# Zero matmuls in more of TensorE's planned gaps, layernorm statistics kept in planned order, and a reordered tail, in a fused attention and FFN kernel

## The chip, the core and the metric

The kernel runs on one core of a Trainium2 chip, as one launch. Its time is the device time of that launch in microseconds (us), lower is better. Five engines share the work, each with its own queue of instructions: TensorE (PE, with its weight loads PEld), VectorE (DVE), ScalarE (ACT), GpSimd (POOL) and SyncE (SP, which here only issues DMAs).

## The reference, cut to what matters

```python
xn = _layernorm(x, axis=-1)            # x: 1 x 2048 x 512, bf16
s = _A_ref(xn, A_wq, A_wk, A_wv, A_wo) # 32 query heads of width 16, one key/value head
g = _silu(_B_ref(xn, B_w_gate, B_w_up, B_w_down))   # SwiGLU FFN, width 1792
return x + s * g

# _A_ref: q = x @ wq (32 heads), k = x @ wk, v = x @ wv
# p = softmax(q k^T / 4) over all 2048 keys; o = p v; o @ wo
# _B_ref: (silu(x @ w_gate) * (x @ w_up)) @ w_down
```

## The kernel before

**The work.** Scores are made transposed, 128 keys by 512 queries, for four heads at once. A pair is 512 queries of eight heads (16 pairs); a pair is done in two blocks of four heads (31 blocks that end with an eviction, and a last one). A block has 16 key tiles. For each tile PE writes scores into two of three two-bank PSUM tiles `ring` (L895), ACT takes the exponential of 1024 columns into a buffer `Pb` (L916, 838 times), and PE adds probabilities times values into `o_ps` (L790). The value weights also hold columns of ones, so `o_ps` carries the softmax's denominators. For 186 of the 1024 half tiles DVE takes the place of ACT: one pass into `Ub` (L928) and, for each two of them, four more passes (L941, L944, L947, L950) whose results `Eb` and `Wb` go into `o_ps` too. At a block's end DVE copies `o_ps` to `oa` (L834), SP sends the denominators to `dn` (L837), and after a pair DVE takes their reciprocal (L724), which goes through DRAM and comes back broadcast as `rb`; POOL multiplies (L735).

**The filling.** The FFN (L654, L674), the queries of the next pair (L515) and the output projection (L690) use a single PSUM bank `m_ps`, one group of matmuls after another, with ACT and DVE work between.

**The order.** It is written by a planner, `_Sched` (L180), at build time: operations carry a cost, dependences and a priority; the planner lets time run, picks for each engine what comes next, and the instructions are emitted in the order of their planned starts. `chain` (L524) then ties each engine's instructions in that order, in one chain per engine. An instruction that is not passed to `chain` is placed by the framework's own scheduler.

**Zero matmuls.** `warm_op` (L739) makes a matmul of a zero weight tile, 512 columns wide, into `o_ps`; it changes no sum. `step` (L255) asks for one when PE would stand idle in the plan for over 0.25 us and the planner's count of PE work over its last `WIN` falls below `LOW`:

```python
if self.warm and start - self.free["PE"] > 0.25 and self.activity(start) < self.LOW:
    ...
    w = self.warm()
    if w is not None and start - max(t, w.ready) > 0.25:
```

`o_rel[0]` is the operation after which `o_ps` may be written anew, which is the block's last copy L834. It is set when the planner comes to the block's last tile (`finish_block`, L825), and until that copy is planned `warm_op` gives nothing.

**The start.** x arrives in tiles of 128 rows. `e_stats` (L436) does the statistics of one tile, BN_STATS (L437) and then BN_AGGR (L438), and returns the second only. Then come the variance plus epsilon (L441), the power -0.5 on POOL (L444), the normalized tile (L455 on DVE for the first four tiles, L451 on POOL for the others), transposes (L466), queries, keys and the first scores.

**The tail.** The last block's four query tiles of 128 rows are finished outside the planner (L995 to L1038), and nothing of that is passed to `chain`: the projection of what is ready (L1002, L1004), the copy of `o_ps` on ACT (L1012), denominators by a matmul (L1015), and for each tile in turn reciprocal, broadcast on DVE, transpose (L1018 to L1021), product (L1022) and the last projection (L1023); then `e_out_mul` (L694), `e_out_add` (L699) and the stores on SP. Last comes a flag (L1031 to L1038): whether all denominators are in range. All engines load it (L1041) and branch over a slower exact path.

## Time and profile before

| what | value |
|---|---|
| time, three runs | 900.57, 905.36, 1078.65 us; median 905.36 us |
| profiled execution, its own time | 903.82 us |
| its span, first to last instruction | 902.0 us |
| mean granted TensorE clock | 0.937 |
| busy: PE, ACT, DVE, POOL | 811.8, 819.9, 711.1, 69.2 us |

The profiled execution lies between the two faster runs. Times in the trace count from the span's start. The granted clock is 1.00 at TensorE's upper level (2.4 GHz) and 0.50 at its lower one (1.2 GHz); for a stretch it is the mean. Matmuls are pipelined and their ends are modelled, so PE's busy time overlaps and is not PE at its peak.

### The profile page before, as it was taken

What the parts mean: (1) busy time and instruction counts of PE and PEld (TensorE: products, weight loads), DVE (VectorE), ACT (ScalarE), POOL (GpSimd) and SP (SyncE); (2) the same over time, 40 slices, a digit from 0 to 9 for tenths busy, and PEclk for the clock granted to TensorE, in tenths of its full rate; (3) what the DMA queues carried; (4) which work ended last, traced back from release to release, by engine and by line L of the source; (5) the groups of instructions that cost most, each with busy time, mean ns of one, the idle gap of its engine ahead of it and who ended that gap; (6) DMA issues with size and microseconds to landing.
All of it is one profiled execution on the core that took longest, in us unless ns stands there. A gap on an engine that the chain in (4) does not pass through costs nothing.

```text
span 902.0 us, 15161 instructions
## 1 busy us (share of the span) xinstructions
PE 811.8 (90%) x5899; PEld 242.2 (27%) x5899; DVE 711.1 (79%) x856; ACT 819.9 (91%) x921; POOL 69.2 (8%) x81
## 2 busy tenths in 40 slices
PE   5899989999989889999999999899998989899984
PEld 2322222222222222222222322222222222222222
DVE  6367887888788996887777988978777998877873
ACT  1999897999999998998989999999998999999981
POOL 4400100000001100000000120000000020000001
PEclk7998896999999997998979999999988999999987
DMA  9200000000000000000000010000000010000000
GB/s 331 66 4 8 12 1 20 1 9 13 4 17 13 25 7 19 2 2 19 1 19 1 13 32 1 19 1 20 2 8 13 7 31 8 19 2 8 13 14 27
DMA packets 20367, 18.78 MB, mean 21 GB/s; under 512 B 9088, under 2 KB 16256, under 8 KB 20288
## 3 DMA queue, kind: packets, MB, share of 16 engines
q1 hardware_dynamic: 18704, 17.18, 6.1%
q8 instruction: 48, 0.79, 0.4%
q10 hardware_dynamic: 1584, 0.56, 0.2%
q14 instruction: 31, 0.25, 0.1%
HBM read 12.88 MB, written 2.36 MB: 17 GB/s over the span
## 4 chain that ended last, share of the span: by engine, by line
PE 43%; ACT 25%; DVE 18%; issue 9%; DMA 2%; SPq 2%; ACTq 0%; DVEq 0%
ACT Pb L916 24%; PE ring L895 17%; PE o_ps L790 11%; DVE Ub L928 7%; PE m_ps L654 6%; PE m_ps L674 4%; DVE Wb L950 2%; DVE Wb L947 2%; SPq L837 2%; DMA dn<-oa 1%; DVE Eb L944 1%; PE o_ps L747 1%; DVE Wb L941 1%; ACT th L659 1%; PE m_ps L690 1%
## 5 line engine op out<-in xcount | busy, mean ns | idle before, releaser
L916 ACT ACTIVATE Pb<-ring 128x1024 bf16<-128x1024 f32 x838 | 790.4, 1085 | 41.1 <-PE ring L895 37.7
L895 PE MATMUL ring<-QB,KT 32*128 32x512 bf16 x2048 | 343.4, 398 | 46.6 <-ACT Pb L916 33.8
L928 DVE TENSOR_SCALAR Ub<-ring 128x1024 uint16<-128x1024 f32 x186 | 227.2, 1222 | 106.9 <-PE ring L895 85.4
L790 PE MATMUL o_ps<-Pb,VA 128*32 128x512 bf16 x1676 | 209.1, 406 | 0.2 <-ACT Pb L916 0.2
L895 PEld LDWEIGHTS <-KT 32*128 32x128 bf16 x2048 | 101.0, 91 | 335.5 <-issue 330.1
L950 DVE TENSOR_TENSOR Wb<-Wb,Ub 128x2048 f16<-128x2048 f16 x93 | 115.1, 1237 | 2.1
L947 DVE TENSOR_TENSOR Wb<-Wb 128x2048 f16<-128x2048 f16 x93 | 114.6, 1232 | 0.0
L790 PE MATMUL o_ps<-Ub,VD 128*32 128x512 f16 x372 | 77.0, 411 | 0.6 <-DVE oa L834 0.4
L654 PE MATMUL m_ps<-xnT,wu_sb 128*128 128x512 bf16 x224 | 71.6, 412 | 3.9 <-DVE ab L661 3.5
L735 POOL TENSOR_TENSOR oT<-oa,rb 128x512 bf16<-128x512 f32 x16 | 24.2, 1511 | 632.2 <-DMA rb<-dscr 491.9
L790 PEld LDWEIGHTS <-VA 128*32 128x32 bf16 x1676 | 50.6, 94 | 81.5 <-issue 81.3
L654 PE MATMUL m_ps<-xnT,wg_sb 128*128 128x512 bf16 x224 | 69.2, 404 | 1.3 <-DVE hT L665 0.6
L674 PE MATMUL m_ps<-wd_sb,hT 128*128 128x512 bf16 x224 | 66.8, 390 | 1.2 <-DVE g_sb L682 0.9
L941 DVE TENSOR_SCALAR Wb<-Ub 128x2048 uint16<-128x2048 uint16 x93 | 65.0, 699 | 1.6
L944 DVE TENSOR_SCALAR Eb<-Ub 128x2048 uint16<-128x2048 uint16 x93 | 64.8, 697 | 0.0
L790 PEld LDWEIGHTS <-VD 128*32 128x32 f16 x1116 | 40.7, 93 | 82.3 <-issue 80.2
L665 DVE TENSOR_TENSOR hT<-ab,m_ps 128x512 bf16<-128x512 f32 x56 | 38.1, 681 | 12.8 <-PE m_ps L654 12.2
L790 PE MATMUL o_ps<-Wb,VD 128*32 128x512 f16 x372 | 38.7, 406 | 7.1 <-DVE Wb L950 6.4
L661 DVE SCALAR_TENSOR_TENSOR ab<-th,m_ps 128x512 f32<-128x512 f32 x56 | 38.1, 681 | 8.7 <-ACT th L659 8.7
L790 PE MATMUL o_ps<-Eb,VD 128*32 128x512 f16 x372 | 38.4, 403 | 7.1 <-DVE Eb L944 6.5
L659 ACT ACTIVATE th<-m_ps 128x512 f32<-128x512 f32 x56 | 36.6, 654 | 4.6 <-PE m_ps L654 4.6
L699 POOL TENSOR_TENSOR xn<-ab,x_sb 128x512 bf16<-128x512 f32 x14 | 20.3, 1450 | 165.7 <-DVE ab L694 165.7
(93 smaller groups left out, 298.3 us busy)
## 6 DMA issues: line engine op xcount, KB each, us to landing
rb<-dscr SPq DMA_DIRECT2D x16, 256.0 KB
out_dram<-xn SPq DMA_DIRECT2D x16, 128.0 KB, 1.7
dn<-oa SPq DMA_DIRECT2D x124, 2.0 KB, 1.7
oa<-oa SPq DMA_DIRECT2D x60, 32.0 KB, 2.0
wg_sb<-in_B_w_gate_dram SPq DMA_DIRECT2D x1, 1792.0 KB, 12.1
wu_sb<-in_B_w_up_dram SPq DMA_DIRECT2D x1, 1792.0 KB
wd_sb<-in_B_w_down_dram SPq DMA_DIRECT2D x1, 1792.0 KB, 19.2
...
```

What stands on the lines that cost most here:

```text
L654: return lambda: [nc.tensor.matmul(out=m_ps[:], lhsT=w[:, kc, f * P:(f + 1) * P], rhs=xnT[:, kc, sc * 512:(sc + 1) * 512], start=(kc == 0) ...
L659: t_ = OP("ACT", 0.48, [a], lambda: nc.scalar.activation(out=th[i][:], in_=m_ps[:], func=ACT.Tanh, scale=0.5), (0,), name="tanh")
L661: s_ = OP("DVE", 0.62, [t_, ab_rel[i]], lambda: nc.vector.scalar_tensor_tensor(out=ab[i][:], in0=th[i][:], scalar=1.0, in1=m_ps[:], op0=AL ...
L674: return lambda: [nc.tensor.matmul(out=m_ps[:, :D], lhsT=hT[:, f, tt * P:(tt + 1) * P], rhs=wd_sb[:, f, :], start=(f == 0), stop=(f == FC ...
L790: r.append(nc.tensor.matmul(out=o_ps[GRP * g:GRP * g + GRP, :], lhsT=lhs, rhs=rhs, start=(n == 0), stop=(n == pv_total[(b, g)] - 1), tile_ ...
L895: return [nc.tensor.matmul(out=ring[sl][:, u * 512:(u + 1) * 512], lhsT=KT[half][GRP * g:GRP * g + GRP, t * P:(t + 1) * P], rhs=QB[pair % ...
L916: ex = OP("ACT", 0.905, [scs[x], pdep, prev_exp], lambda i=i, sl=sl: nc.scalar.activation(out=Pb[i][:], in_=ring[sl][:], func=ACT.Exp, sca ...
L928: pa = OP("DVE", 1.16, [scs[dx]] + udep, lambda ui=ui, x=dx, sl=sl: nc.vector.tensor_scalar(out=Ub[ui][:, x * 1024:(x + 1) * 1024], in0=ri ...
L941: e1 = OP("DVE", 0.62, [pa, pa0, edep], lambda ui=ui, ei=ei: nc.vector.tensor_scalar(out=Wb[ei][:], in0=Ub[ui][:], scalar1=0x3FF, scalar2= ...
L944: e2 = OP("DVE", 0.62, [pa, pa0, edep], lambda ui=ui, ei=ei: nc.vector.tensor_scalar(out=Eb[ei][:], in0=Ub[ui][:], scalar1=0x7C00, scalar2 ...
L947: e3 = OP("DVE", 1.18, [e1], lambda ei=ei: nc.vector.tensor_tensor(out=Wb[ei][:].bitcast(FP16), in0=Wb[ei][:].bitcast(FP16), in1=Wb[ei][:] ...
L950: e4 = OP("DVE", 1.18, [e3], lambda ui=ui, ei=ei: nc.vector.tensor_tensor(out=Wb[ei][:].bitcast(FP16), in0=Wb[ei][:].bitcast(FP16), in1=Ub ...
```

## The change

There are four edits. (1) `LOW` goes from 3300 to 3600. (2) `warm_op` gives a zero matmul also between `finish_block` and the block's copy: into `o_ps` while some of the block's matmuls are still to come, and, when they are all planned, into `m_ps` if a group of matmuls there is begun and not ended. `finish_block` hands the last block's matmuls to the same test. (3) `e_stats` and `e_flag1` return all their instructions, so that all of them are chained. (4) The tail is written in another order and chained: the copy of `o_ps` is split between ACT and DVE, the broadcasts go to ACT, reciprocals and products take two tiles at once, the flag is worked out before the outputs, and two of the four stores are issued from ACT.

```diff
-    WIN, LOW = 3.0, 3300
+    WIN, LOW = 3.0, 3600
...
     def e_stats(n):
-        nc.vector.bn_stats(out=stats[:, n, :], in_=x_sb[:, n, :])
-        return nc.vector.bn_aggr(out=mv[:, n, :], in_=stats[:, n, :])
+        return [nc.vector.bn_stats(out=stats[:, n, :], in_=x_sb[:, n, :]),
+                nc.vector.bn_aggr(out=mv[:, n, :], in_=stats[:, n, :])]
...
     def grp_pe(parts, prio, paced=False):
...
+        grp = []
+        m_cur.append(grp)
+        while m_cur[0] and m_cur[0][-1].start is not None:
+            m_cur.pop(0)
...
             last = sd.add(o)
+            grp.append(o)
...
     def warm_op():
         ev = o_rel[0]
-        if ev.start is None:
-            return None
+        rdy = 0.0
+        dst = o_ps
+        if ev.start is not None:
+            rdy = ev.end + sd.LAT["DVE"]
+        elif all(d.start is not None for d in ev.deps if d.eng == "PE"):
+            if not any(len(f_) > 1 and f_[0].start is not None and f_[-1].start is None for f_ in m_cur):
+                return None
+            dst = m_ps
...
-            st_ = not any(acc_open)
-            return nc.tensor.matmul(out=o_ps[:], lhsT=zeros_w[:], rhs=KT[0][:, 0:512] if late else QB[1][:],
+            st_ = dst is o_ps and not any(acc_open)
+            return nc.tensor.matmul(out=dst[:], lhsT=zeros_w[:], rhs=KT[0][:, 0:512] if late else QB[1][:],
...
         if b == 2 * NPAIR - 1:
             st["last_pv"] = pvs
-            o_rel[0] = _Op("EXT", 0.0, [], None, (0,))
+            o_rel[0] = _Op("EXT", 0.0, [p_ for p_ in pvs], None, (0,))
...
+    t_acc(0)
+    chain("ACT", nc.scalar.copy(out=oe[:, qsl(0, 2)], in_=o_ps[:, qsl(0, 2)]))
+    chain("DVE", nc.vector.tensor_copy(out=oe[:, qsl(2, 2)], in_=o_ps[:, qsl(2, 2)]))
     for i in range(4):
...
+        t_dq(i)
+    t_acc(1)
+    t_rec(0, 2)
+    t_rec(2, 2)
...
     for i in range(4):
...
+        t_rdx(i)
+    t_rq(0)
+    t_rq(1)
+    t_acc(2)
+    t_rq(2)
+    t_rq(3)
+    t_mul(0, 2)
+    chain("PE", nc.tensor.transpose(out=m_ps[0:1, 0:P], in_=fmin[:, 3:4], identity=ident_f[:]))
+    t_acc(3)
+    t_mul(2, 2)
     for i in range(4):
...
+        t_wom(i)
...
+    chain("DVE", nc.vector.tensor_single_scalar(out=flag_i[:], in_=fm2[0:1, 0:1], scalar=0.5, op=ALU.is_lt))
     for i in range(4):
+        chain("DVE", e_out_mul(NL + i, accs[i], tmps[i]))
+    for i in range(4):
+        pool_ = i < 2
+        chain("POOL" if pool_ else "DVE", e_out_add(NL + i, tmps[i], nc.gpsimd if pool_ else nc.vector))
+        q_ = "SP" if i % 2 == 0 else "ACT"
```

In the new tail `t_acc` is the projection of what is ready for one query tile (four matmuls, as L1002 and L1004), `t_dq` the denominators (L1015), `t_rec` the reciprocal (L1018), `t_rdx` the broadcast (L1019, now on ACT), `t_rq` its transpose (L1021), `t_mul` the product (L1022) and `t_wom` the last projection (L1023).

In the whole program before the exact path PE has 94 zero matmuls before the change and 187 after it. All 187 write `o_ps`; none writes `m_ps`. The changed kernel's line numbers are up to 46 higher.

**DVE at the start.** From the first variance operation to the first normalized tile, before:

```order
L441 TENSOR_SCALAR veps<-mv 128x2
L437 BN_STATS stats<-x_sb 128x6
L441 TENSOR_SCALAR veps<-mv 128x2
L438 BN_AGGR mv<-stats 128x2 x2
L437 BN_STATS stats<-x_sb 128x6 x2
L351 TENSOR_SCALAR hbit<-pidx 128x1
L437 BN_STATS stats<-x_sb 128x6
L353 TENSOR_SCALAR hmask<-hbit 128x1
L354 TENSOR_SCALAR hmask<-hbit 128x1
L437 BN_STATS stats<-x_sb 128x6 x4
L455 TENSOR_SCALAR xn_116<-x_sb,mv,rstd 128x512
```

The same stretch of DVE after the change:

```order
L441 TENSOR_SCALAR veps<-mv 128x2 x2
L437 BN_STATS stats<-x_sb 128x6
L438 BN_AGGR mv<-stats 128x2
L437 BN_STATS stats<-x_sb 128x6
L438 BN_AGGR mv<-stats 128x2
L351 TENSOR_SCALAR hbit<-pidx 128x1
L353 TENSOR_SCALAR hmask<-hbit 128x1
L354 TENSOR_SCALAR hmask<-hbit 128x1
L455 TENSOR_SCALAR xn_116<-x_sb,mv,rstd 128x512
```

Eight BN_STATS stood between the first variance operation and the first normalized tile, and two stand there now; the six others come later, in pairs, between the copies of the transposes.

**PE at a block's end.** The scores of a new block (`KT_84` with `QB_120`) just ahead of the last product of the block that ends (`Pb_126`), at the place that the trace of before has at 344.8 us; before:

```order
L895 LDWEIGHTS KT_84
L895 MATMUL ring_98<-QB_120,KT_84 128x512
L895 LDWEIGHTS KT_84
L895 MATMUL ring_96<-QB_120,KT_84 128x512
L895 LDWEIGHTS KT_84
L895 MATMUL ring_96<-QB_120,KT_84 128x512
L790 LDWEIGHTS VA
L790 MATMUL o_ps<-Pb_126,VA 32x512
```

The same place of PE after the change:

```order
L907 LDWEIGHTS KT_84
L907 MATMUL ring_98<-QB_120,KT_84 128x512
L759 LDWEIGHTS zeros_w
L759 MATMUL o_ps<-KT_84,zeros_w 128x512
L759 LDWEIGHTS zeros_w
L759 MATMUL o_ps<-KT_84,zeros_w 128x512
L907 LDWEIGHTS KT_84
L907 MATMUL ring_96<-QB_120,KT_84 128x512
```

Two zero matmuls stand between the two pairs of score matmuls, where none stood.

**DVE in the tail.** From the product of the third query tile to the flag, before:

```order
L1022 TENSOR_TENSOR oT_151<-oa_143,ring_98 128x128
L1031 TENSOR_SCALAR rb_144<-ring_98 128x16
L1032 TENSOR_TENSOR rb_144<-rb_144,ring_98 128x16
L694 SCALAR_TENSOR_TENSOR oa_140<-ring_97,g_sb 128x512
L694 SCALAR_TENSOR_TENSOR oa_141<-ring_97,g_sb 128x512
L699 TENSOR_TENSOR xn_118<-oa_140,x_sb 128x512
L699 TENSOR_TENSOR xn_119<-oa_141,x_sb 128x512
L1033 TENSOR_REDUCE fmin<-rb_144 128x1
L1034 TENSOR_REDUCE fmin<-fmin 128x1
L1037 TENSOR_REDUCE fm_8151<-m_ps 1x1
L1038 TENSOR_SCALAR flag_i<-fm_8151 1x1
```

And DVE after the change, from the two products to the end of the tail:

```order
L1043 TENSOR_TENSOR oT_151<-oa_143,ring_98 128x256 x2
L1075 TENSOR_REDUCE fm_8183<-m_ps 1x1
L1076 TENSOR_SCALAR flag_i<-fm_8183 1x1
L700 SCALAR_TENSOR_TENSOR ab_138<-ring_96,g_sb 128x512
L700 SCALAR_TENSOR_TENSOR ab_139<-ring_96,g_sb 128x512
L700 SCALAR_TENSOR_TENSOR oa_140<-ring_97,g_sb 128x512
L700 SCALAR_TENSOR_TENSOR oa_141<-ring_97,g_sb 128x512
L705 TENSOR_TENSOR xn_118<-oa_140,x_sb 128x512
L705 TENSOR_TENSOR xn_119<-oa_141,x_sb 128x512
```

The flag is now ahead of the output products and sums, and the last work of DVE is the last sum.

## Rows read from the trace of the kernel before

**Rows 1.** The page: span; granted clock in 40 equal slices, in tenths.

```profile
span 902.0 us, 15161 instructions
...
PEclk7998896999999997998979999999988999999987
```

**Rows 2.** Groups by line: shapes, count | busy us, mean ns | idle before, releaser.

```profile
L916 ACT ACTIVATE Pb<-ring 128x1024 bf16<-128x1024 f32 x838 | 790.4, 1085 | 41.1 <-PE ring L895 37.7 <-PE o_ps L790 1.9 <-ACT Pb L916 0.3
...
L747 PE MATMUL o_ps<-KT,zeros_w 128*128 128x512 bf16 x74 | 28.8, 412 | 0.0
```

**Rows 3.** Half-clock windows: length, busy by engine (instructions), clock, DMA share, GB/s.

```profile
348.00:361.60 13.60, 13.60 (x65) 2.47 (x63) 9.57 (x13) 10.14 (x11) 1.27 (x1) 0.50 0.12 31
...
409.40:416.20 6.80, 6.80 (x34) 1.02 (x32) 3.41 (x4) 2.38 (x4) 1.26 (x1) 0.50 0.16 46
...
860.00:866.80 6.80, 6.45 (x35) 1.22 (x34) 4.47 (x5) 2.67 (x4) 1.27 (x1) 0.50 0.13 41
sum 88.80, PE 88.45 PEld 15.96 DVE 61.78 ACT 61.08 POOL 9.64; mean PE 11.06 PEld 2.00 DVE 7.72 ACT 7.64 POOL 1.20
```

**Rows 4.** Windows between those, at full clock, from 95.4 to 860 us: sum of seven.

```profile
sum 696.30, PE 636.07 PEld 193.31 DVE 583.07 ACT 682.43 POOL 34.75; mean PE 90.87 PEld 27.62 DVE 83.30 ACT 97.49 POOL 4.96
```

**Rows 5.** Timeline of PE, then DVE, at one block's end: start, us, what [idle before].

```profile
344.76 0.39 PE L895 MATMUL ring<-QB,KT 32*128 32x512 bf16 x2
346.06 0.39 PE L895 MATMUL ring<-QB,KT 32*128 32x512 bf16 x2 [0.91 <-ACT Pb L916]
...
348.28 0.68 DVE L834 COPY oa<-o_ps 128x512 f32<-128x512 f32 x1
```

**Rows 6.** Timeline at two places where PE waits longer: DVE, PE, DVE.

```profile
407.97 0.35 DVE L724 RECIPROCAL rc<-dn 128x32 f32<-128x32 f32 x1 [2.01 <-DMA dn<-oa]
...
408.92 0.40 PE L790 MATMUL o_ps<-Eb,VD 128*32 128x512 f16 x4 [1.75 <-DVE Eb L944]
...
859.40 0.35 DVE L724 RECIPROCAL rc<-dn 128x32 f32<-128x32 f32 x1 [2.78 <-DMA dn<-oa]
```

**Rows 7.** Who waited for whom, whole span: us in total, times, longest.

```profile
PE ring L895 <- ACT Pb L916: 33.8, 108, 1.0
```

**Rows 8.** Timeline at the start: DVE, POOL, ACT.

```profile
11.84 2.46 DVE L437 BATCH_NORM_STATS2 stats<-x_sb 128x6 f32<-128x512 bf16 x4
14.22 1.37 DVE L455 TENSOR_SCALAR xn<-x_sb,mv,rstd 128x512 bf16<-128x512 bf16 x4
...
9.26 1.40 POOL L444 TENSOR_TENSOR rstd<-veps,neg_half 128x2 f32<-128x2 f32 x2 [4.15 <-DVE veps L441]
...
16.54 1.01 POOL L444 TENSOR_TENSOR rstd<-veps,neg_half 128x4 f32<-128x4 f32 x1 [5.87 <-DVE veps L441]
...
22.65 7.44 ACT L916 ACTIVATE Pb<-ring 128x1024 bf16<-128x1024 f32 x8 [2.47 <-PE ring L895]
```

**Rows 9.** Timeline of the tail, all engines.

```profile
881.73 0.39 PE L790 MATMUL o_ps<-Pb,VA 128*32 128x512 bf16 x2
...
884.87 0.95 PE L1015 MATMUL ring<-sel,oa 128*128 128x4 f32 x8
...
887.37 0.23 DVE L1019 COPY oa<-rc 128x128 f32<-128x128 f32 x1
...
887.65 0.49 PE L1021 MATMUL ring<-ident_f,oa 128*128 128x128 f32 x2
...
889.85 2.26 POOL L699 TENSOR_TENSOR xn<-ab,x_sb 128x512 bf16<-128x512 f32 x2 [23.41 <-DVE ab L694]
...
890.49 0.60 DVE L1019 COPY oa<-rc 128x128 f32<-128x128 f32 x1
...
893.04 1.29 DVE L694 SCALAR_TENSOR_TENSOR oa<-ring,g_sb 128x512 f32<-128x512 f32 x2 [0.41 <-PE ring L1023]
894.24 1.28 DVE L699 TENSOR_TENSOR xn<-oa,x_sb 128x512 bf16<-128x512 f32 x2
...
896.58 0.14 DVE L1038 TENSOR_SCALAR flag_i<-fm 1x1 int32<-1x1 f32 x1
```

More of the change, by code (lines that the diff above doesn't have):

```diff
@@ L563 @@
     npaced = [0]
+    m_cur = []
     def grp_pe(parts, prio, paced=False):
@@ L750, in warm_op @@
         o.left = 0
-        o.ready = ev.end + sd.LAT["DVE"]
+        o.ready = rdy
         return o
@@ L998 @@
     qpar = (NSC - 1) % 2
-    for i in range(4):
-        n = NL + i
-        for jj in range(jl):
-            nc.tensor.matmul(out=accs[i], lhsT=oT[qpar][:, jj, i * P:(i + 1) * P], rhs=wo_sb[:, jj, :],
-                             start=(jj == 0), stop=False)
-        nc.tensor.matmul(out=accs[i], lhsT=oT[qpar][:, jl, i * P:(i + 1) * P], rhs=wom[0][:],
-                         start=(jl == 0), stop=False)
     oe = oa[3]
@@ L1034, with qsl @@
-    nc.vector.tensor_reduce(out=fmin[:, 3:4], in_=fmin[:, 0:3], axis=AX.X, op=ALU.min)
-    nc.tensor.transpose(out=m_ps[0:1, 0:P], in_=fmin[:, 3:4], identity=ident_f[:])
-    fm2 = sb([P, 2], FP32, "fm2")
-    nc.vector.tensor_reduce(out=fm2[0:1, 0:1], in_=m_ps[0:1, 0:P], axis=AX.X, op=ALU.min)
-    nc.vector.tensor_single_scalar(out=flag_i[:], in_=fm2[0:1, 0:1], scalar=0.5, op=ALU.is_lt)
+    tmps = [ab[0], ab[1], oa[0], oa[1]]
+    fl = rb[0]
+    fm2 = sb([P, 2], FP32, "fm2")
+    def qsl(i, n=1):
+        return slice(i * P, (i + n) * P)
@@ new lines, in t_acc, with t_dq @@
+    def t_acc(i):
+        for jj in range(jl):
+            chain("PE", nc.tensor.matmul(out=accs[i], lhsT=oT[qpar][:, jj, qsl(i)], rhs=wo_sb[:, jj, :],
+                                         start=(jj == 0), stop=False))
+        chain("PE", nc.tensor.matmul(out=accs[i], lhsT=oT[qpar][:, jl, qsl(i)], rhs=wom[0][:],
+                                     start=(jl == 0), stop=False))
+    def t_dq(i):
+        chain("PE", nc.tensor.matmul(out=dq[:, 4 * i:4 * i + 4], lhsT=oe[:, qsl(i)], rhs=sel[:], start=True, stop=True))
@@ new lines, in t_rec, with t_rdx, t_rq @@
+    def t_rec(i, n):
+        chain("DVE", nc.vector.reciprocal(out=rd4[:, 4 * i:4 * (i + n)], in_=dq[:, 4 * i:4 * (i + n)]))
+    def t_rdx(i):
+        chain("ACT", nc.scalar.copy(out=oa[2][:, qsl(i)].rearrange("p (g r) -> p g r", r=GRP),
+                                    in_=rd4[:, 4 * i:4 * i + 4].rearrange("p (g o) -> p g o", o=1).to_broadcast(
+                                        [P, 4, GRP])))
+    def t_rq(i):
+        chain("PE", nc.tensor.matmul(out=rq[:, qsl(i)], lhsT=oa[2][:, qsl(i)], rhs=ident_f[:], start=True, stop=True))
@@ new lines, in t_mul, with t_wom @@
+    def t_mul(i, n):
+        chain("DVE", nc.vector.tensor_tensor(out=oT1[:, qsl(i, n)], in0=oe[:, qsl(i, n)], in1=rq[:, qsl(i, n)],
+                                             op=ALU.mult))
+    def t_wom(i):
+        chain("PE", nc.tensor.matmul(out=accs[i], lhsT=oT1[:, qsl(i)], rhs=wom[1][:], start=False, stop=True))
+    t_acc(0)
+    chain("ACT", nc.scalar.copy(out=oe[:, qsl(0, 2)], in_=o_ps[:, qsl(0, 2)]))
+    chain("DVE", nc.vector.tensor_copy(out=oe[:, qsl(2, 2)], in_=o_ps[:, qsl(2, 2)]))
@@ new lines @@
+    for i in range(4):
+        t_dq(i)
+    t_acc(1)
+    t_rec(0, 2)
+    t_rec(2, 2)
+    chain("DVE", nc.vector.tensor_scalar(out=fl[:, 0:16], in0=dq, scalar1=DEN_LO, scalar2=DEN_HI,
+                                         op0=ALU.max, op1=ALU.min))
+    chain("DVE", nc.vector.tensor_tensor(out=fl[:, 16:32], in0=fl[:, 0:16], in1=dq, op=ALU.is_equal))
+    chain("DVE", nc.vector.tensor_reduce(out=fmin[:, 2:3], in_=fl[:, 16:32], axis=AX.X, op=ALU.min))
+    chain("DVE", nc.vector.tensor_reduce(out=fmin[:, 3:4], in_=fmin[:, 0:3], axis=AX.X, op=ALU.min))
@@ new lines @@
+    for i in range(4):
+        t_rdx(i)
[8 more added lines that the diff above has]
+    t_mul(2, 2)
+    for i in range(4):
+        t_wom(i)
+    chain("DVE", nc.vector.tensor_reduce(out=fm2[0:1, 0:1], in_=m_ps[0:1, 0:P], axis=AX.X, op=ALU.min))
+    chain("DVE", nc.vector.tensor_single_scalar(out=flag_i[:], in_=fm2[0:1, 0:1], scalar=0.5, op=ALU.is_lt))
@@ L1039 @@
+    for i in range(4):
+        chain("DVE", e_out_mul(NL + i, accs[i], tmps[i]))
[3 more added lines that the diff above has]
+        q_ = "SP" if i % 2 == 0 else "ACT"
+        n = NL + i
+        chain(q_, (nc.sync if q_ == "SP" else nc.scalar).dma_start(out=out_v[:, n, :], in_=res[n % 4][:, :D]))
     MAIN.close()
```

26 lines of the change are left out of this document (3 added, 23 removed).

## The prediction

> **What bounds the kernel now.** I read the page's slices and granted clock first, then the groups by line, then windows cut where the clock changes, then the timeline just ahead of each fall, at last the start and the tail.
>
> ACT is the bound: its exponentials alone are busy 790.4 us of the span of 902.0, and nearly all of their idle time, 37.7 us, is waiting for score matmuls [rows 1, 2]. The slices show where: the clock's digit is 9 (90% or more) in most and 6 to 8 in some [rows 1]. Cut at the changes of the clock, there are eight stretches at half clock between 81 and 867 us, 88.8 us in all. In them ACT is busy for 61.08 us, so it idles 27.7 us [rows 3]. In the stretches at full clock it is busy 682.43 of 696.3 us and idles 2.0% [rows 4]. So the low clock costs ACT 27.7 - 1.8 = 25.9 us, nearly all that there is to win in the middle of the kernel. PE is busy for every microsecond of such a stretch but part of the last: there PE is the bound.
>
> What comes before a fall differs. Six of the eight begin within 4 us of a block's end, like the one at 348.0. There PE has only single pairs of score matmuls and waits for ACT between them: 0.91 us ahead of the pair at 346.06, with the block's copy at 348.28 [rows 5]. The two others, at 409.4 and 860.0, follow waits for a DMA: the reciprocal of the denominators holds DVE for 2.01 and 2.78 us, and PE waits 1.75 us for `Eb` behind it [rows 6]. The idle time of these two is 4.42 + 4.13 = 8.55 us [rows 3], 8.3 above the 2%. The six have the remaining 17.6.
>
> At the start ACT has its first exponential at 22.65 us, and DVE works through statistics right up to the first normalized tile at 14.22 [rows 8]. After the last product (to 882.12) a chain of small steps follows to the flag at 896.72, and 5.3 us of loading the flag and branching to the end [rows 1, 9].
>
> **The change part by part.** The sum is made against the profiled execution's own time of 903.82 us (span and 1.8 us around it), which is 1.5 us below the median of 905.36.
>
> *Zero matmuls.* The program gets 93 more. All go to `o_ps`: the new way into `m_ps` is never used, so that part of the edit does nothing. I went through the six block ends in the new order: zeros now stand at each, two in the shown place right in the wait of 0.91 us. I take it that they hold the clock at five of the six, since one that stands a little beside the wait may not help, and since other block ends are as thin as these: 5/6 of 17.6 is 14.7 us. The two waits for a DMA stay. The planner does not see them, so hardly a zero is put there. I give them a quarter of their 8.3 us, 2.1, for the last one, where the new order has one more DVE operation ahead of the reciprocal. Together -16.8 us. Ends: 0, if the clock falls as often elsewhere; -25.9, if no stretch is left.
>
> The zeros' own cost: each is 412 ns by its group [rows 2], so 93 would be 38 us if each one held up a score matmul that was ready. They stand where PE waits. PE's score matmuls waited for ACT 33.8 us in 108 waits [rows 7], which is the cover; and a wait of 0.91 us takes two. If a wait is shorter than planned, the zero delays the next scores by what is left. I take +1 us, nearer to the covered end, since the shown row has its wait where the order has the zeros; the range is 0 to +38.
>
> The rule that speaks against it is in the Trainium skill, "TensorE: Matmul & The Clock Gate", section "Part 3: Packing small matmuls — row/col tiling": matmuls start and end strictly in program order. No row of mine shows a matmul overtaken. By that rule alone a zero that comes late is paid in full, towards +38; by the row of the wait it is paid in part, and the sum keeps +1.
>
> *Statistics in order.* Before the first normalized tile DVE now has six BN_STATS fewer. Four took 2.46 us, so six take 3.7, and 14.22 could become 10.5. POOL's power operations end only at 9.26 + 1.40 = 10.66 [rows 8], so at most 3.5 us are gained there. Some is given back: the six, now each with its BN_AGGR, stand between the copies that the next keys and values need. Of the second chunk three come before its variance: after xn at 10.7 + 1.4 and three tiles at 0.7, the power operation starts at 14.3 to 14.7, not 16.54, 1.8 to 2.2 us earlier. What is late next is the value path, which the first products wait for. I take -2.2 us, the value that the second chunk bears out; range 0 to -3.5.
>
> *The tail.* Before, the denominators' matmuls wait until PE has done about three groups of projections, 882.12 to 884.87, and then four rounds run one after another until 893.04 [rows 9]. Now one group of four matmuls (0.9 us, an estimate from those 2.75 us for three) hides the copies, and the denominators end at 882.12 + 0.9 + 0.95 = 884.0. Then PE has three groups (2.7), four transposes at 0.49 (2.0), the flag's (0.4) and the first last projection (0.2), with reciprocals, broadcasts and products hidden beside the groups: 889.3. Four output products at 0.65 (1.29 for two) and two sums (1.28) give 893.2. The 5.3 us from DVE's last operation to the end stay, since every engine still loads the flag behind its own last work: 898.5 and not 902.0, -3.5 us. If the stores on ACT or a broadcast on ACT come late it is -2; if the branch of the engines that are done early hides some of the 5.3 us, -6.
>
> One thing may eat into it. DVE's broadcast took 0.60 us beside POOL's sums and 0.23 without them [rows 9]. The Trainium skill, "SBUF — State Buffer", section "SBUF: two separate sides", says that POOL and a DVE operation with two inputs in SBUF exclude each other for the whole instruction. By that rule DVE's two last sums wait for POOL's second, which would end about 0.4 us after DVE is ready: -3.1 instead of -3.5. The sum keeps -3.5.
>
> Sum: 903.82 - 16.8 + 1 - 2.2 - 3.5 = 882.3 us, told as 882.
>
> **The rivals.**
>
> *The clock falls as often, at other places.* Only six places are known from one execution, and at other block ends the clock stayed up with the same thin work, so the rows don't tell why one falls and the next does not. Moved zeros and a start that is 2 us earlier shift everything. Against it: the zeros are at all six ends, and from about 474 to 669 us the clock held, eight slices of 9 in a row [rows 1], through seven block ends without the new ones. Time: 903.82 - 2.2 - 3.5 = 898.1 us.
>
> *All stretches go, with the two after DMA waits.* For it: there too a zero more stands near. Against it: 1.75 us of PE waiting is longer than any wait at a block's end [rows 5, 6]. Time: 903.82 - 25.9 - 2.2 - 3.5 = 872.2 us.
>
> *Slower: the zeros hold up the scores.* PE keeps its order, so a zero that starts when ACT has just freed `ring` delays the pair behind it, and ACT with it, at each block. With the clock gain lost too, the time is 898.1 plus 0.412 a zero: above 905.4 from 18 of the 93 on, 923.5 with 62, 936 with all. For it: PE is busy for the whole of each half-clock stretch, where a zero has no cover [rows 3]. Against it: PE waits for ACT 33.8 us in all [rows 7], and 74 zeros there already leave ACT short of scores hardly at all at full clock [rows 2, 4].
>
> **How the numbers follow.** Forecast 0.60, clock falls elsewhere 0.26, all stretches go 0.08, slower 0.06. The forecast's own range is 874 to 890: three to all of the six held, and the smaller terms at their ends. The range must reach the second case at 898 and nearly the third: 867 (all clock losses gone, the smaller terms at their better ends, 903.8 - 25.9 - 3.5 - 6 = 868.4) to 899; what is left out is most of the slower case and a part of the second. A measurement tells about 2% from no change: 887.3 us or less is faster, above 923.5 slower. The forecast lies below 887.3 with 0.55 of its 0.60, the third case with its 0.08, and the second with 0.02: faster 0.65. Slower needs 62 delaying zeros: 0.03. The same: 0.32.
>
> **What would show it right or wrong.** Right: the slices show full clock but for about three places; the stretches that remain follow a reciprocal's wait for `dn`; ACT idles under 25 us between its first and last exponential; the first exponential starts near 20.4 us; 16 to 17 us pass from the last product to the end. Wrong: as many slices with a low clock as before, or a wait of ACT for scores with a zero matmul right ahead of them at full clock. If the first normalized tile starts at 11 us and the first products as late as before, the start's term is wrong; if the time from DVE's last sum to the end grows over 5.3 us, the tail's.

## The result, and the profile after

The changed kernel takes 878.78 us (median of four runs, 876.5 to 882.01), the kernel before, in the runs beside it, 906.12 (four too, one of them 1078.65). The ratio is 0.9721 with a 95% interval of 0.9662 to 0.9779: faster by 2.8%. Medians here and below are over all runs of a kernel, while a ratio is taken over the runs within 1.5% of the kernel's fastest, which leaves out many with much time at half clock, so it need not be the quotient of two medians.

The profiled execution after took 882.01 us (span 880.2), 21.8 us less than the one before. This is the page of the changed kernel, in the parts that answer to [rows 1, 2]; in its group rows, busy time and mean ns stand behind the count, then the idle time before them and what ended it. The exponential is now L928 (before L916), the scores L907, the products L802, the zero matmuls L759 (the trace kept 138 of the 165 behind the start):

```profile
span 880.2 us, 15242 instructions
...
PEclk9899999999999999999999899999999989999987
...
L928 ACT ACTIVATE Pb<-ring 128x1024 bf16<-128x1024 f32 x838 | 791.5, 1090 | 30.8 <-PE ring L907 26.5
...
L962 DVE TENSOR_TENSOR Wb<-Wb,Ub 128x2048 f16<-128x2048 f16 x93 | 116.5, 1252 | 1.9
...
L759 PE MATMUL o_ps<-KT,zeros_w 128*128 128x512 bf16 x138 | 49.4, 400 | 1.6 <-issue 1.6
```

ACT's work is the same to 1 us. Its waiting for scores went from 37.7 to 26.5 us. The slices show a clock under 9 in five of 40, where eleven were.

Cut at the changes of the clock, the changed kernel has five stretches at half clock between the first exponential and the last product. From 80 us on there are three with 27.3 us, where eight held 88.8 us before [rows 3]; ahead of that are two, where one of 3.4 us was (at 30.5). Columns as there:

```profile
34.20:41.10 6.90, 6.68 (x39) 2.09 (x38) 1.28 (x3) 5.30 (x6) 0.00 (x0) 0.51 0.02 5
44.50:47.90 3.40, 3.18 (x21) 0.88 (x20) 0.05 (x1) 1.94 (x2) 1.16 (x4) 0.50 0.02 5
498.50:505.30 6.80, 6.80 (x35) 1.48 (x34) 5.61 (x6) 3.55 (x4) 1.27 (x1) 0.50 0.12 39
706.70:713.50 6.80, 6.47 (x33) 1.06 (x33) 4.50 (x7) 5.28 (x6) 0.00 (x0) 0.50 0.11 23
850.00:863.70 13.70, 13.03 (x65) 2.57 (x63) 6.04 (x7) 10.07 (x11) 0.00 (x0) 0.50 0.00 0
sum 37.60, PE 36.16 PEld 8.08 DVE 17.49 ACT 26.14 POOL 2.42; mean PE 7.23 PEld 1.62 DVE 3.50 ACT 5.23 POOL 0.48
...
sum 788.50, PE 721.76 PEld 222.20 DVE 668.55 ACT 770.91 POOL 41.38; mean PE 240.59 PEld 74.07 DVE 222.85 ACT 256.97 POOL 13.79
```

The last row is the sum of the three windows at full clock, from 47.9 to 850 us: ACT idles 17.6 of 788.5 us there, 2.2%, where it was 2.0% [rows 4]. In the five at half clock it idles 37.6 - 26.14 = 11.5 us, of which 27.3 - 18.9 = 8.4 in the last three, instead of 27.7.

At a block's end, the place that answers to [rows 5], the timeline of PE (and one row of DVE) now reads:

```profile
334.68 0.61 PE L759 MATMUL o_ps<-KT,zeros_w 128*128 128x512 bf16 x2
...
335.65 0.39 PE L907 MATMUL ring<-QB,KT 32*128 32x512 bf16 x2 [0.37 <-ACT Pb L928]
...
337.88 0.68 DVE L846 COPY oa<-o_ps 128x512 f32<-128x512 f32 x1
```

Two zeros stand in the wait and leave 0.37 us of its 0.91; the clock stayed up there. What comes before the three falls that remain in the middle differs, as the timeline shows at 498.5, 706.7 and 850.0:

```profile
495.74 0.35 DVE L730 RECIPROCAL rc<-dn 128x32 f32<-128x32 f32 x1 [1.47 <-DMA dn<-oa]
...
498.49 0.62 PE L802 MATMUL o_ps<-Wb,VD 128*32 128x512 f16 x4 [1.30 <-DVE Wb L962]
...
704.66 1.31 PE L907 MATMUL ring<-QB,KT 32*128 32x512 bf16 x6 [0.91 <-ACT Pb L928]
...
704.94 0.68 DVE L846 COPY oa<-o_ps 128x512 f32<-128x512 f32 x1
...
845.80 1.49 POOL L741 TENSOR_TENSOR oT<-oa,rb 128x512 bf16<-128x512 f32 x1 [23.76 <-DMA rb<-dscr]
...
846.20 2.17 DVE L962 TENSOR_TENSOR Wb<-Wb,Ub 128x2048 f16<-128x2048 f16 x1
...
848.42 0.40 PE L802 MATMUL o_ps<-Wb,VD 128*32 128x512 f16 x4 [1.27 <-DVE Wb L962]
```

The first follows a reciprocal that waited for `dn`, as [rows 6] did. The second is a block's end with the old wait of 0.91 us and no zero in it. The third follows a DVE operation that took 2.17 us beside a product on POOL (its mean is 1.25 by the page). The list of waits of the changed kernel (us in total, times, longest), against [rows 7]:

```profile
ACT Pb L928 <- PE ring L907: 26.5, 49, 2.9
PE ring L907 <- ACT Pb L928: 24.2, 95, 0.9
...
DVE rc L730 <- DMA dn<-oa: 14.2, 14, 1.5
...
PE o_ps L802 <- DVE Wb L962: 10.3, 16, 1.4
```

The start, against [rows 8] (POOL, DVE, POOL, ACT):

```profile
6.95 1.41 POOL L444 TENSOR_TENSOR rstd<-veps,neg_half 128x2 f32<-128x2 f32 x2 [1.82 <-DVE veps L441]
...
10.24 1.38 DVE L455 TENSOR_SCALAR xn<-x_sb,mv,rstd 128x512 bf16<-128x512 bf16 x4
...
14.16 1.01 POOL L444 TENSOR_TENSOR rstd<-veps,neg_half 128x4 f32<-128x4 f32 x1 [5.81 <-DVE veps L441]
...
18.26 4.69 ACT L928 ACTIVATE Pb<-ring 128x1024 bf16<-128x1024 f32 x5 [2.88 <-PE ring L907]
```

The first power operation starts 2.31 us earlier, the first normalized tile 3.98, the second power operation 2.38 and the first exponential 4.39. And the tail, against [rows 9]:

```profile
863.17 0.62 PE L802 MATMUL o_ps<-Pb,VA 128*32 128x512 bf16 x4
...
869.24 0.75 DVE L1043 TENSOR_TENSOR oT<-oa,ring 128x256 bf16<-128x256 f32 x2 [2.75 <-PE ring L1025]
...
870.22 0.14 DVE L1076 TENSOR_SCALAR flag_i<-fm 1x1 int32<-1x1 f32 x1
...
871.20 2.26 POOL L705 TENSOR_TENSOR xn<-ab,x_sb 128x512 bf16<-128x512 f32 x2 [23.91 <-DVE ab L700]
...
872.77 1.84 DVE L705 TENSOR_TENSOR xn<-oa,x_sb 128x512 bf16<-128x512 f32 x2
873.49 1.51 ACTq L1084 DMA_DIRECT2D out_dram<-xn  x2
```

From the end of the last product (863.79) to the end of the span 16.4 us pass, where it was 902.0 - 882.12 = 19.9.

**A line through the runs.** One execution of each kernel says little about the clock, since it differs from run to run. Every run lists its span and its mean granted clock; with two levels, span x (1 - clock) x 2 is the time that it spent at half clock. The kernel before had 65 to 171 such us in the 55 runs beside these experiments, 110 in the mean, and the runs lie on a line: span = 866.4 + 0.318 x half-clock us, with 1.4 us of scatter (one standard deviation). The slope is the price of a microsecond at half clock; [rows 3, 4] gave 25.9 / 88.8 = 0.29. So each kernel has two numbers that tell its effects apart: its mean half-clock time, and how far its runs lie off that line, which is what it does beside the clock. Within the kernels with ten runs or more the slope is 0.32 to 0.39, so the line carries over roughly: with a slope of 0.35 the changed kernel would lie 1.1 us above it and not 1.2 below, so a distance far from 110 us at half clock is good to about 2 us. For the changed kernel: 37.7 us at half clock, and 1.2 us below the line.

### The profile page after: what moved, and what is told of

It reads as the page before. It is cut to its first block, busy times and chain, and to the rows that moved or that the text cites. A ratio compares the mean times of both kernels' runs of the same rounds, so it can differ in the third digit from the quotient of the medians.

```text
span 880.2 us, 15242 instructions
## 1 busy us (share of the span) xinstructions
PE 792.1 (90%) x5890; PEld 247.3 (28%) x5992; DVE 714.8 (81%) x849; ACT 819.8 (93%) x922; POOL 67.6 (8%) x81
## 4 chain that ended last, share of the span: by engine, by line
PE 35%; DVE 28%; ACT 20%; issue 9%; DMA 4%; SPq 3%; DVEq 0%; POOL 0%; ACTq 0%; POOLq 0%
ACT Pb L928 19%; PE ring L907 14%; DVE Ub L940 9%; PE o_ps L802 9%; PE m_ps L660 4%; DVE Wb L962 4%; PE m_ps L680 4%; DVE Wb L959 3%; SPq L849 3%; DVE Eb L956 2%; DMA dn<-oa 2%; DVE Wb L953 2%; PE o_ps L759 2%; DVE oa L846 1%; DVE ab L667 1%
## 5 line engine op out<-in xcount | busy, mean ns | idle before, releaser
L928 ACT ACTIVATE Pb<-ring 128x1024 bf16<-128x1024 f32 x838 | 791.5, 1090 | 30.8 <-PE ring L907 26.5
L907 PE MATMUL ring<-QB,KT 32*128 32x512 bf16 x2048 | 332.4, 387 | 40.9 <-ACT Pb L928 24.2
L802 PE MATMUL o_ps<-Pb,VA 128*32 128x512 bf16 x1676 | 203.3, 398 | 0.0
L907 PEld LDWEIGHTS <-KT 32*128 32x128 bf16 x2048 | 99.7, 91 | 307.3 <-issue 300.6
L959 DVE TENSOR_TENSOR Wb<-Wb 128x2048 f16<-128x2048 f16 x93 | 116.8, 1255 | 0.0
L802 PE MATMUL o_ps<-Ub,VD 128*32 128x512 f16 x372 | 73.2, 393 | 0.8 <-DVE oa L846 0.7
L802 PEld LDWEIGHTS <-VA 128*32 128x32 bf16 x1676 | 50.1, 94 | 80.6 <-issue 80.5
L660 PE MATMUL m_ps<-xnT,wu_sb 128*128 128x512 bf16 x208 | 63.2, 386 | 4.1 <-DVE ab L667 2.2
L802 PEld LDWEIGHTS <-VD 128*32 128x32 f16 x1116 | 42.5, 93 | 82.0 <-issue 79.5
L680 PE MATMUL m_ps<-wd_sb,hT 128*128 128x512 bf16 x204 | 61.0, 383 | 2.6 <-issue 2.1
L660 PE MATMUL m_ps<-xnT,wg_sb 128*128 128x512 bf16 x197 | 60.2, 386 | 2.0 <-issue 1.2
L759 PE MATMUL o_ps<-KT,zeros_w 128*128 128x512 bf16 x138 | 49.4, 400 | 1.6 <-issue 1.6
L802 PE MATMUL o_ps<-Wb,VD 128*32 128x512 f16 x372 | 37.8, 395 | 11.2 <-DVE Wb L962 10.3
L802 PE MATMUL o_ps<-Eb,VD 128*32 128x512 f16 x372 | 37.6, 393 | 6.0 <-DVE Eb L956 4.1
## 6 DMA issues: line engine op xcount, KB each, us to landing
wd_sb<-in_B_w_down_dram SPq DMA_DIRECT2D x1, 1792.0 KB, 19.9
```

The lines of the kernel that those rows point to most:

```text
L660: return lambda: [nc.tensor.matmul(out=m_ps[:], lhsT=w[:, kc, f * P:(f + 1) * P], rhs=xnT[:, kc, sc * 512:(sc + 1) * 512], start=(kc == 0) ...
L680: return lambda: [nc.tensor.matmul(out=m_ps[:, :D], lhsT=hT[:, f, tt * P:(tt + 1) * P], rhs=wd_sb[:, f, :], start=(f == 0), stop=(f == FC ...
L759: return nc.tensor.matmul(out=dst[:], lhsT=zeros_w[:], rhs=KT[0][:, 0:512] if late else QB[1][:], start=st_, stop=st_)
L802: r.append(nc.tensor.matmul(out=o_ps[GRP * g:GRP * g + GRP, :], lhsT=lhs, rhs=rhs, start=(n == 0), stop=(n == pv_total[(b, g)] - 1), tile_ ...
L907: return [nc.tensor.matmul(out=ring[sl][:, u * 512:(u + 1) * 512], lhsT=KT[half][GRP * g:GRP * g + GRP, t * P:(t + 1) * P], rhs=QB[pair % ...
L928: ex = OP("ACT", 0.905, [scs[x], pdep, prev_exp], lambda i=i, sl=sl: nc.scalar.activation(out=Pb[i][:], in_=ring[sl][:], func=ACT.Exp, sca ...
```

## The experiments

This table has them all: median of n runs; ratio to the kernel before in the runs beside it, with interval; mean half-clock time; mean distance from the line. The medians of the kernel before were 904.56 us beside `e1`, `e2`, `e3` and `e6`, 903.66 beside `e4`, `e5`, `e7` and `e8`, and 899.36 beside the four `f` runs.

| Run | Median us (n) | Ratio | Half clock us | Off the line us |
|---|---|---|---|---|
| changed kernel | 878.78 (4) | 0.9721 [0.9662, 0.9779] | 37.7 | -1.2 |
| e1_zeros: edits 1, 2 | 896.1 (4) | none given | 71.7 | +4.3 |
| e2_stats: edit 3 | 886.26 (4) | 0.984 [0.9686, 0.9994] | 71.9 | -3.4 |
| e3_tail: edit 4 | 899.66 (10) | 0.9965 [0.9895, 1.0036] | 104.6 | -1.8 |
| e6_narrow | 901.7 (6) | 0.9882 [0.9751, 1.0014] | 121.4 | -7.6 |
| e4_low: edit 1 | 893.85 (10) | 1.0007 [0.9944, 1.007] | 82.2 | +1.8 |
| e5_rule: edit 2 | 906.17 (4) | 1.0171 [1.0004, 1.0339] | 94.0 | +6.9 |
| e7_double | 887.55 (10) | 0.9941 [0.9879, 1.0002] | 24.1 | +11.6 |
| e8_dma | 865.51 (5) | 0.9684 [0.942, 0.9949] | 34.5 | -9.8 |
| f1_stats: edit 3 again | 887.84 (12) | 0.9874 [0.9831, 0.9917] | 77.7 | -2.1 |
| f2_zeros_tail: edits 1, 2, 4 | 896.09 (12) | 0.9957 [0.9915, 1.0] | 77.6 | +3.0 |
| f4_stats_tail: edits 3, 4 | 889.34 (6) | 0.9871 [0.9808, 0.9935] | 78.7 | -5.0 |
| f3_dma_w256 | 877.52 (6) | 0.9668 [0.9584, 0.9752] | 68.3 | -10.2 |

The half-clock time of the kernel before scatters by 23 us from run to run (one standard deviation), so a mean of four runs is good to some 12 us and one of twelve to 7. The intervals of `e3_tail`, `e4_low`, `e6_narrow`, `e7_double` and `f2_zeros_tail` reach 1.0 or pass it: their ratios alone show no change of time, and what follows rests on the two columns on the right.

**Each part alone.** The first three put the edits of the change into the kernel before, one by one. `e1_zeros` has edits 1 and 2, the zeros:

```diff
-    WIN, LOW = 3.0, 3300
+    WIN, LOW = 3.0, 3600
...
-        if ev.start is None:
-            return None
+        rdy = 0.0
+        dst = o_ps
...
-            o_rel[0] = _Op("EXT", 0.0, [], None, (0,))
+            o_rel[0] = _Op("EXT", 0.0, [p_ for p_ in pvs], None, (0,))
```

> The kernel before with edits 1 and 2 alone (187 zero matmuls; statistics and tail as before). Clock theory: this edit carries most of the gain; the eight half-clock stretches between 81 and 867 us (88.8 us) shrink to two to four (under 35 us), ACT's idle time inside them from 27.7 to under 11 us, and the time is 886 to 892 us. Rival (start and tail carry it): 900 us or more.

`e2_stats` has edit 3 (its part in `e_flag1`, of the same kind, is left out here):

```diff
-        nc.vector.bn_stats(out=stats[:, n, :], in_=x_sb[:, n, :])
-        return nc.vector.bn_aggr(out=mv[:, n, :], in_=stats[:, n, :])
+        return [nc.vector.bn_stats(out=stats[:, n, :], in_=x_sb[:, n, :]),
+                nc.vector.bn_aggr(out=mv[:, n, :], in_=stats[:, n, :])]
```

> The kernel before with edit 3 alone. The first exponential starts at 18.3 us instead of 22.65. Theory A (the gain at the start is kept to the end): 902 us. Theory B (it is given back within the first two blocks, since half-clock stretches come into the start when the early score matmuls run beside less other work): the first block's copy at 55 us as before, time 904 to 907 us.

`e3_tail` has edit 4:

```diff
+    chain("ACT", nc.scalar.copy(out=oe[:, qsl(0, 2)], in_=o_ps[:, qsl(0, 2)]))
+    chain("DVE", nc.vector.tensor_copy(out=oe[:, qsl(2, 2)], in_=o_ps[:, qsl(2, 2)]))
...
```

> The kernel before with edit 4 alone. From the last product's end to the span's end 16.4 us instead of 19.9, time 902 to 903 us (3.5 us less than before). Rival: the tail's gain in the changed kernel needs the earlier clock, and here it is under 1.5 us.

The zeros alone took the half-clock time from 110 to 72 us, which is worth 38 x 0.318 = 12 us, and lie 4.3 us above the line. Between 81 and 867 us the profiled execution of `e1_zeros` has 13.6 us at half clock, less than the 35 that were expected at most, but the median of 896.1 us fits neither of its two expectations. The tail alone lies 1.8 us under the line and leaves the clock as it was; in its profiled execution 15.5 us pass from the last product to the end, where 16.4 were expected. The statistics alone are the surprise: 3.4 us below the line, near the price that they were given, but 38 us less at half clock as well, though they add no work to PE. Neither theory expected that. The page has a low clock at the start and at the end; between them the trace has only three falls of 3.4 us (at 59.8, 162.2 and 288.5):

```profile
span 882.8 us, 15060 instructions
...
PEclk8589999999999999999999999999999999999976
```

Four runs are few for that, so `f1_stats` repeats it below.

**Is it the zeros' work that holds the clock?** `e6_narrow` is the changed kernel with the same zeros in the same places, only 64 columns wide:

```diff
-            return nc.tensor.matmul(out=dst[:], lhsT=zeros_w[:], rhs=KT[0][:, 0:512] if late else QB[1][:],
+            return nc.tensor.matmul(out=dst[:, 0:64], lhsT=zeros_w[:], rhs=KT[0][:, 0:64] if late else QB[1][:, 0:64],
```

> The changed kernel with the same 187 zero matmuls at the same places, but 64 columns wide instead of 512. Clock theory: it is the work of the zeros that holds the clock, so at least six half-clock stretches of 3 us or more stand between 81 and 850 us again, and the time is 893 to 905 us. Rival (the gain is from order and spacing of the instructions): 877 to 882 us as for the changed kernel.

The page of `e6_narrow`, and its group of zeros:

```profile
span 896.8 us, 15248 instructions
...
PEclk9876999999999999999999899899997999997957
...
L759 PE MATMUL o_ps<-KT,zeros_w 128*128 128x64 bf16 x165 | 26.3, 205 | 0.0
```

The half-clock time is back at 121 us, with PE's and ACT's instructions in the same order. So what holds the clock is what the zeros do on PE, not the order that the planner makes around them. The zeros that the kernel before has are narrow here too, so 121 us is to be held against the 79 of `f4_stats_tail`, which has those 94 at full width and no others. This kernel is 7.6 us below the line, 6.4 under the changed one: that is what the zeros' full width costs over these narrow ones, of 165 x (400 - 205) ns = 32 us that they take longer.

**The two halves of the zeros' edit, their number, and the other wait.** `e4_low` has only the new `LOW` (149 zeros, 55 more than before), `e5_rule` only the new rule of `warm_op` (116 zeros, 22 more):

```diff
-    WIN, LOW = 3.0, 3300
+    WIN, LOW = 3.0, 3600
```

> The kernel before with LOW 3600 alone: 149 zero matmuls, 55 more. Over 13 runs of the kernel before, the span is 868.0 us + 0.309 us for each us at half clock, within 1.1 us. Theory (half clock and the zeros' own price are separate terms): the zeros bring the time at half clock from 109 us (mean of before) to 65 to 90, and cost 2 to 4 us beyond that line, since 93 cost about 3 to 6; span 890 to 899 us. Rival (zeros are free): on the line within 1 us.

```diff
-        if ev.start is None:
-            return None
+        rdy = 0.0
+        dst = o_ps
+        if ev.start is not None:
+            rdy = ev.end + sd.LAT["DVE"]
...
```

> The kernel before with the new warm_op alone (LOW 3300): 116 zero matmuls, 22 more, most of them ahead of a block's copy, where six of the eight falls of the profiled run were. Theory (the place counts more than the number): the time at half clock falls to 60 to 85 us and the price is 1 us or less beyond the line; span 887 to 895 us. Rival (the number counts): half clock over 95 us, span 897 us or more.

The number alone gives most of what the two give together: 82 us at half clock against 72, at +1.8 us off the line, though its ratio of 1.0007 shows no gain in time. The rule alone is no gain, close to the rival that the number counts: 94 us at half clock, and 6.9 us above the line, which is most of what the 22 zeros take at their mean of 404 ns (8.9 us), though 55 cost 1.8 in `e4_low`. The list of its waits names another one, PE waiting for DVE to have read the scores, 16.5 us where the kernel before has 8.4:

```profile
PE ring L908 <- DVE Ub L941: 16.5, 39, 2.4
```

But `e2_stats` and `e6_narrow` have 13.1 and 14.9 us of the same wait and lie below the line, so it does not explain the price, and the cause stays open.

`e7_double` is the changed kernel with each zero after the start sent twice (352 for 187):

```diff
-            return nc.tensor.matmul(out=dst[:], lhsT=zeros_w[:], rhs=KT[0][:, 0:512] if late else QB[1][:],
-                                    start=st_, stop=st_)
+            return [nc.tensor.matmul(out=dst[:], lhsT=zeros_w[:], rhs=KT[0][:, 0:512] if late else QB[1][:],
+                                     start=st_, stop=st_) for _ in range(2 if late else 1)]
```

> The changed kernel with each of the 165 later zero matmuls given twice. Theory (a zero has a price of about 0.06 us, as 93 cost 5.6 us in the changed kernel beyond the line, against the one with narrow zeros): half clock 20 to 45 us, 9 to 12 us more beyond the line, span 881 to 890 us. Rival (the zeros stand in idle time and are free): span 870 to 876 us, as the clock falls less often.

The clock then hardly falls between start and end, and the cover is used up: PE waits for ACT 11.2 us instead of 24.2, and ACT waits more for scores.

```profile
PEclk8999999999999999999999999999999999999998
...
L928 ACT ACTIVATE Pb<-ring 128x1024 bf16<-128x1024 f32 x838 | 792.6, 1073 | 34.2 <-PE ring L907 30.0
```

```profile
PE ring L907 <- ACT Pb L928: 11.2, 47, 0.9
```

The 165 more zeros cost 11.6 + 1.2 = 12.8 us, 0.078 each, and win back 13.6 us at half clock, worth 4.3. The median is 8.8 us worse than the changed kernel's. So a fifth of each second zero is paid, and clock and price have a best point between.

`e8_dma` is the changed kernel with one number more changed, the planner's price of the denominators' DMA, so that it plans the reciprocal later:

```diff
-        d = OP("DMA", 2.4, [ev], dens, (0,))
+        d = OP("DMA", 4.4, [ev], dens, (0,))
```

> The changed kernel with the planner's price for the denominators' DMA at 4.4 us instead of 2.4, so that the reciprocal (and what waits behind it on DVE) is planned after the data is there. Theory (the falls that are left come from waits that the planner doesn't see): DVE waits under 4 us for the denominators in all instead of 14.2, half clock between 50 and 850 us under 15 us instead of 27, span 870 to 876 us. Rival (the falls that are left are at block ends and from shared ports): the waits go but the time at half clock does not, 876 to 881 us.

The wait of the reciprocal for `dn`, 14.2 us, is gone from the list of waits, and with it PE's for `Wb` shrinks from 10.3 to 4.1 and ACT's for scores from 26.5 to 19.1:

```profile
PE ring L907 <- ACT Pb L928: 24.5, 86, 0.9
...
ACT Pb L928 <- PE ring L907: 19.1, 43, 2.6
...
PE o_ps L802 <- DVE Wb L962: 4.1, 9, 1.0
```

It is the fastest version: 865.51 us, below both kernels. Yet the half-clock time is about the changed kernel's (34.5 and 37.7 us). The gain is 8.6 us off the line: the waits themselves, not the falls behind them. Neither expectation held in full. In the profiled execution one fall, from 99.7 to 123.6 us, makes up 23.9 of some 45 us at half clock, and from there to 864 us there is none, where the changed kernel had three; `f3_dma_w256` has the same fall at 97.8, and what starts it is open. Four of the five runs of `e8_dma` are below all of the changed kernel's; against the kernel before the interval of its ratio reaches 0.9949, so by how much it is faster is open.

**The statistics again, and the rest without them.** `f1_stats` is `e2_stats` once more. `f2_zeros_tail` has edits 1, 2 and 4, `f4_stats_tail` edits 3 and 4 (their diffs are those above put together), and `f3_dma_w256` is `e8_dma` with zeros half as wide:

```diff
-            return nc.tensor.matmul(out=dst[:], lhsT=zeros_w[:], rhs=KT[0][:, 0:512] if late else QB[1][:],
+            return nc.tensor.matmul(out=dst[:, 0:256], lhsT=zeros_w[:], rhs=KT[0][:, 0:256] if late else QB[1][:, 0:256],
```

> The kernel before with edit 3 alone, once more, for the spread of its time at half clock: four runs gave 46 to 104 us (mean 72) against 65 to 171 (mean 110) in 32 runs of the kernel before, though TensorE's order is the same. Theory (chance of four runs beyond a start that loses 5 to 8 us less at half clock): mean of half clock 90 to 110 us, median time 892 to 898 us. Rival (the earlier start alone takes away falls in the middle): mean 60 to 80 us, 882 to 889 us.

> The changed kernel without edit 3 (edits 1, 2 and 4: 187 zero matmuls, new tail, statistics as before). If the statistics give about 4 us and little of the clock: half clock 45 to 70 us, 881 to 888 us. Rival (the statistics carry most of the gain): half clock over 70 us, 890 us or more.

> The changed kernel without the zeros (edits 3 and 4 alone, 94 zero matmuls). If the zeros carry most of the clock gain: half clock 85 to 110 us, 888 to 896 us. Rival (statistics carry it): half clock under 75 us, 882 us or less.

> The version with the DMA's price at 4.4 us (865.5 us median of five) and zero matmuls 256 columns wide instead of 512. If a zero's price goes with its width and half the width still holds the clock: 860 to 864 us. If the narrower zeros hold it less: half clock over 45 us and 866 us or more.

Edit 3 alone holds over twelve runs: 77.7 us at half clock, ratio 0.9874. Without it, zeros and tail give 0.9957 only, 896.09 us; with it, the changed kernel's 878.78. The page of `f1_stats` shows a low clock where the kernel before had one near 348 and 409, and none at 460 and 668:

```profile
span 884.4 us, 15161 instructions
...
PEclk8799999999999996998999999999999999999997
```

In the middle its waits are those of before: PE waited for ACT 32.3 us there and 33.8 before [rows 7]:

```profile
PE ring L895 <- ACT Pb L916: 32.3, 104, 1.0
```

For `f4_stats_tail` neither expectation fits: 79 us at half clock is below the range of the one and 889.34 us above that of the other. The half-width zeros are a miss: 68 us at half clock for 34.5, and no lower a price (-10.2 against -9.8 off the line).

The half-clock time thus adds up about as the distances do. From 110 us the zeros take 38, the statistics 32 to 38 and the tail 5, together 75 to 81; the change took 72. Taken out of pairs that have the tail, the zeros give 27 and 41 us and the statistics 26 and 40, so neither has much the larger share. Off the line they give +4.3, -2.1 to -3.4 and -1.8, together +0.4 to -0.9, and the change has -1.2.

## Why the prediction was right, and where its parts were not

The total was 882.0 us and the measured median 878.78, inside the range; faster by over 2%, as the likeliest case said. The split behind it was not right: by the line nearly the whole gain is clock, and the other three terms cancel. The profiled executions spent 902.0 x 0.063 x 2 = 113.7 and 880.2 x 0.027 x 2 = 47.5 us at half clock; the difference is worth 66.2 x 0.318 = 21.1 us of the 21.8. So it is luck that this execution, at 882.01 us, lies within 0.3 us of the sum: the clock brought 4.3 us more than its term, and the other three, -4.7 us in the sum, brought 4.0 less than theirs.

**What bounds the kernel** was read rightly. ACT's work stayed, and its idle time came down where PE runs at half clock, 27.7 to 8.4 us in the stretches from 80 us on, while its 2% at full clock did not move.

**The clock term, -16.8 us,** was too small and had the wrong owner. In the profiled pair it measured -21.1; over all runs it is (110 - 37.7) x 0.318 = -23. The step that failed is the one that gave all of it to the zeros: alone they are worth 12 us (`e1_zeros`), and the statistics, which the sum priced only by their path, bring 10 to 12 more (`e2_stats`, `f1_stats`). The mechanism itself was right: the clock fell without the zeros' width (`e6_narrow`), and a wait with two zeros in it kept its clock. That a block's end here and there would still fall was right too: 706.7. "The stretches that remain follow a reciprocal's wait for `dn`" held for one of three; another followed the end without a zero, the third a slow DVE operation. And the sum left out the stretch from the first exponential to 80 us, where the changed kernel has 6.9 + 3.4 us at half clock and the kernel before 3.4 (ahead of the first exponential it is 3.4 and 10.3). Most of the start's gain was given back there in this execution: the first product starts 3.7 us earlier (26.79, before 30.46), the first block's copy 0.4 (55.4, before 55.8).

**The zeros' price, +1 us,** was too low. Three pairs give it for the 93: the zeros alone are 4.3 us off the line, zeros with tail stand at +3.0 against -1.8 for the tail, and the change at -1.2 against -5.0 for statistics with tail: 4.3, 4.8 and 3.8. That is 0.045 us each, a ninth of a zero's duration (0.058 with a slope of 0.35 for the line). The step that failed took the shown block's end for the normal case. The sign that the prediction named for this stands in the trace, at full clock: ACT waits for scores that PE starts right behind two zeros.

```profile
816.74 0.60 PE L759 MATMUL o_ps<-KT,zeros_w 128*128 128x512 bf16 x2
817.27 0.39 PE L907 MATMUL ring<-QB,KT 32*128 32x512 bf16 x2
...
817.76 1.02 ACT L928 ACTIVATE Pb<-ring 128x1024 bf16<-128x1024 f32 x1 [0.41 <-PE ring L907]
```

Six such waits, with no idle time of PE between zeros and scores, stand in this execution, 2.1 us in all; not all of that need be the zeros' doing. The Trainium skill's rule that matmuls start and end in program order ("TensorE: Matmul & The Clock Gate", "Part 3: Packing small matmuls — row/col tiling"), which the prediction weighed against its row, points the right way: with the cover used up in `e7_double` a zero costs 0.078 us. By that rule alone, +38, the price would have been far off; nearly all of it is covered.

**The statistics, -2.2 us,** had about the right size for their own part: -2.1 and -3.4 off the line alone, -3.2 and -4.2 in the pairs that have the tail. But the bound was wrong. The prediction held that POOL's power operations end at 10.66 us and that the first normalized tile could not start before. It starts at 10.24, since the power operations themselves start at 6.95. In the order of before a BN_STATS, of a tile whose load was still on its way, stood ahead of the first variance operation, and another between the two; now both variances (at 6.73 us) go ahead of the one that waits. Before, then after:

```profile
8.35 0.69 DVE L437 BATCH_NORM_STATS2 stats<-x_sb 128x6 f32<-128x512 bf16 x1 [1.57 <-DMA x_sb<-in_A_x_dram]
...
8.34 0.69 DVE L437 BATCH_NORM_STATS2 stats<-x_sb 128x6 f32<-128x512 bf16 x1 [1.33 <-DMA x_sb<-in_A_x_dram]
```

The move of the statistics was followed for DVE and not for what waits behind it on POOL. The first exponential starts at 18.26 and not near 20.4.

**The tail, -3.5 us,** measured -3.5 in the profiled pair. Off the line the tail alone gives -1.8 only; the rest lies in the line's other number, since PE has no work at the end and the clock is low there (from 890.7 us on before, 11.3 us to the end; from 873.9 after, 6.3 us; 5 x 0.318 = 1.6). The rule that DVE with two inputs in SBUF and POOL exclude each other (the Trainium skill, "SBUF — State Buffer", "SBUF: two separate sides") fits the rows: DVE's two sums took 1.84 us beside POOL's instead of 1.28 without them, 0.56 where the prediction reckoned 0.4. The end had room for it elsewhere: the flag's last operation now starts 2.55 us before DVE's last two sums. And the 5.3 us behind DVE's last operation did not quite stay: from the last sum's end (874.61) it is 5.6, which is the prediction's own sign of an error in this term, a small one. It was made up before it, since that sum ends 10.8 us after the last product and the prediction reckoned 11.1.

**What was to be seen.** The slices behind the start are low at three places, as said, and at the end. ACT was to idle under 25 us between its first and last exponential; it idled 31.1, of which 11.5 at half clock, 17.6 at full clock in the middle and 2 in the start. 16 to 17 us from the last product to the end: 16.4.

**The rivals.** "All stretches go" did not happen. "The clock falls as often, at other places" did not either, though it is what the kernel with narrow zeros does: 121 us at half clock, 901.7 us. The slower one is real as a mechanism and small: it costs about 4 us for the 93 and 12.8 more for a second zero in each gap, and even `e7_double` is not slower than before.

**What stays open.** Why an earlier start takes clock falls away 400 us later is not shown. The order of PE, ACT and POOL is the same with and without edit 3. DVE's differs behind the start at two places only, near 98 and 867 us of the trace of before, where one pass moves ahead of a flag's operations (`e_flag1`, which edit 3 chains as well). The thin waits for ACT are nearly the same (33.6 us in `e2_stats`, 32.3 in `f1_stats`, 33.8 before). In the single executions the stretches of before at 348.0, 378.7 and 409.4 come again in `f1_stats` at 339.4, 370.2 and 400.9, at the same exponentials, while those at 81.7, 460.6 and 668.8 do not; the one at 81.7 is back in `f4_stats_tail`, at 79.6. That the same program has from 65 to 171 us at half clock suggests that small shifts decide many of the falls; what in edit 3 shifts them for the better was not tried apart.
